# One dK store in two parts, over two DMA queues

## Chip, cores and metric

The kernel runs on one core of a Trainium2 chip. The metric is the device time of one execution in microseconds (us); the median of three runs before the change is 1361.11 us (1361.1 to 1362.07). The core has a matrix engine (PE), a vector engine (DVE), a scalar engine (ACT), GpSimd (POOL) and a sync engine (SP) that here does little but issue transfers. Transfers between HBM and on-chip memory (SBUF, 128 partitions) are moved by 16 DMA engines.

## The reference

One decode step of a transformer block with adaptive layer norm, and its gradients. The part that sets the time is attention of one query per head over a cache: 32 heads, 8192 positions, head size 192, bf16.

```python
scores = jnp.einsum('bhqd,bhkd->bhqk', q, k) * Dh ** (-0.5)
p = _softmax(scores, axis=-1)
o = jnp.einsum('bhqk,bhkd->bhqd', p, v)
...
_out, _vjp = jax.vjp(_f, A_x, A_k_cache, A_v_cache, A_wq, A_wo, B_w3, B_w4, c, w_mod)
_grads = _vjp(grad_out)
```

The outputs include the gradients of both caches, dK and dV, each as large as its cache: 32 heads of 8192 x 192 numbers, 3 MB (3072 KB) per head. Per head dV is the outer product of the probabilities p and the gradient `do` of o, and dK that of dS and q, where dS comes from p and the product of V with `do`. Beside that there are the gradients of the projections `wq` and `wo`, of the MLP's `w3` and `w4`, of the modulation's weights `w_mod`, and three outputs of 640 numbers.

## The kernel before

A head's K, V, dK or dV lies in SBUF as 128 partitions of 64 positions each; one partition's row is 64 x 192 bf16 = 24,576 bytes, and contiguous in HBM. "Half" tiles of 32 positions are used where a buffer is smaller (1536 KB, rows of 12,288 bytes).

The forward stage (to about 545 us) goes over the heads 0 to 31. It loads K and V of each head, computes scores on DVE and PE (`fwd_mult`, `fwd_ssum`), the softmax on ACT and DVE, and sums over the positions on PE. It never normalizes V's product by a second pass: `fwd_kv` keeps matrices (L471, L482) from which the gradient of q is later read. L488 (`fwd_kvK`) multiplies with `hot_bf`, a small constant tile with one column of ones; no line after the forward stage reads it.

A middle stage (545 to 565 us) does the MLP forward and backward; here the DMA queues drain.

The backward stage goes over the heads from 31 down: `HS[i] = 31 - i`, one iteration i of the loop at L1465 per head. V is loaded again (`ring_load`, L880) into one of two places of `v_mem`. In iteration i:

- `bwd_dv` makes dV of the next head: ACT the first 20 positions of each half (L1243), DVE the rest (L1219), then the store at L1265.
- `bwd_mult` multiplies V by `do` on DVE (L131) and sums on PE (L1238).
- `bwd_ds` makes dS, and `bwd_dk` makes dK: two DVE multiplies (L1219) and the store at L1283.
- Jobs are mixed in: gradients of `wo`, `w4`, `w3` (L1301 to L1314) and, over the iterations 10 to 24, of `wq` and `w_mod` (L1332 load, L1354 multiply, L1355 store).

Output tiles of 3 MB take turns in three places A, B and C of `k_mem`; later the places X and V1 join them:

```python
outs += list("BCA") * 11 + ["B"]
outs += ["X", "C", "A", "B"] * 2 + ["X", "C", "V1", "B", (0, 1)]
st2 = nc.sync
```

A place is written again three outputs later, so ACT at L1243 and DVE at L1219 wait until its old content has been stored. All loads and stores of the backward stage are issued by SP, in program order; an SP instruction that waits for its data holds up all later ones. Each DMA marks its completion on one of eight semaphores in turn, and an issue waits until the DMA eight issues earlier has landed.

PE, DVE and ACT run their instructions in the order in which the program emits them (`pin_order`); GpSimd and SP are not pinned, and the recording layer orders them. GpSimd has ten short instructions in the whole kernel; the last two rebuild `sel_bf` (L1460, L1461) after L1206 has read it, for L1130, which first reads it at 610.3 us.

Of the kernel before, what the change touches and what calls it, by code (L numbers as in the profile page):

```python
# [20 lines left out]
def kernel(  # L21
# [26 lines left out]
    nc = tc.nc  # L48
# [16 lines left out]
    P = 128  # L65
# [34 lines left out]
    def bank_c(name):  # L100
        return bank("c", CB[0], name)
# [9 lines left out]
    hot_bf = const.tile([P, 2 * HQ - 1], BF16, name="hot_bf")  # L111
# [78 lines left out]
    def dve_copy(out, in_):  # L190
        nc.vector.tensor_copy(out=out, in_=in_)
# [10 lines left out]
    dK_hd = [out_2[0, h].rearrange("(p j) d -> p j d", p=P) for h in range(HQ)]  # L202
# [449 lines left out]
    for i in range(1, HQ):  # L652
        c, p, pp = 2 <= i < HQ, 0 <= i - 1 < HQ, 0 <= i - 2 < HQ
# [192 lines left out]
    HS = list(range(HQ - 1, -1, -1))  # L846
# [22 lines left out]
    def ring_load(i):  # L869
        if i == 2:  # L870
            load_wo(1, v_tile(bv, 5))
        while v_jobs and all(("v", HS[v_occ[sl][0]], v_occ[sl][1]) in freed for sl in range(v_jobs[0][2], v_jobs[0][2] + v_jobs[0][3])):
            k, t, slot, n = v_jobs.pop(0)
            for r in range(n):
                v_occ[slot + r] = (k, t + r)
            if n == 1:
                V_b.setdefault(HS[k], {})[t] = load_v(fv, HS[k], t, slot)
            else:
                V_b[HS[k]] = {r: v_tile(fv, slot + r) for r in range(2)}
                nc.sync.dma_start(out=v_pair(k), in_=V_hd[HS[k]])  # L880
        for n in W_AT.get(i, ()):
            name, u, use = W_USE[n]
            load_side(name, u, v_tile(bv, 5) if n % 3 == 0 else side["w"].tile([P, JH, DH], BF16, name="W_sb", tag=f"sw{n % 3}"))

    def out_place(k):
        if isinstance(k, tuple):
            return [big_half(x) for x in k], None
        tl = places[k]
        return [tl[:, 0:JH, :], tl[:, JH : 2 * JH, :]], tl
# [15 lines left out]
    st2 = nc.sync  # L905
# [13 lines left out]
    def bwd_pf(h):  # L919
        bwd_pf_act(h)  # L920
        bwd_pf_dve(h)
# [188 lines left out]
    def bwd_wo_red(b):  # L1110
        ps, lo, n = dof_ps.pop(b)
        nc.vector.reduce_sum(out=dof[:, 3 * lo : 3 * (lo + n)], in_=ps, axis=AX.X)
# [7 lines left out]
    def fin_do_sum(b):  # L1120
        lo, n = PS[BATCHES[b][-1]], len(BATCHES[b])
        bwd_wo_red(b)
        sl = slice(3 * lo, 3 * (lo + n))
        dop = bsm.tile([P, 9], BF16, name="dop")[:, 0 : 3 * n]
        dve_copy(dop, dof[:, sl])
        ps = bank_c("dop_ps")
        for k in range(3):
            for c in range(3):
                lo2 = 2 + k * P - c
                nc.tensor.matmul(ps[:, k * n : (k + 1) * n], lhsT=sel_bf[:, lo2 : lo2 + P], rhs=dop[:, c : 3 * n : 3], start=(c == 0), stop=(c == 2))  # L1130
        do_rows[b] = (sl, ps, n)
# [57 lines left out]
    def bwd_dob(hp):  # L1189
        do_pb[hp] = pair_bc(bsm, do_bf, hp, "do_pb")  # L1190
        q_pb[hp] = pair_bc(bsm, q_bf, hp, "q_pb")
# [26 lines left out]
    def pairs_outer(o, pairs, vec, n):  # L1218
        nc.vector.tensor_tensor(  # L1219
            out=o.rearrange("p j (d r) -> p j d r", r=2),  # L1220
            in0=pairs[:, :, None, :].to_broadcast([P, n, NP2, 2]),
            in1=vec.rearrange("p (d r) -> p d r", r=2)[:, None, :, :].to_broadcast([P, n, NP2, 2]),
            op=ALU.mult)

    def vec_of(d, h):
        return d[h // 2][:, (h % 2) * DH : (h % 2 + 1) * DH]

    def bwd_mult(h, t, parts=1):
        if t == 0:
            w = SB[0] // J  # L1230
            bst[h]["dP_ps"] = bank("s", 2, "dP_ps", SB[0]).rearrange("p (j d) -> p j d", d=w)
        w = SB[0] // J
        n = JH // parts
        for r in range(0, JH, n):
            V_sb = V_b[h][t][:, r : r + n, :]
            mul(V_sb, V_sb, vec_of(do_pb, h)[:, None, :].to_broadcast([P, n, DH]))
            for k in range(DH // w):
                nc.tensor.matmul(bst[h]["dP_ps"][:, t * JH + r : t * JH + r + n, :], lhsT=ident_bf, rhs=V_sb[:, :, k * w : (k + 1) * w], start=(k == 0), stop=(k == DH // w - 1))  # L1238
        freed.add(("v", h, t))
# [34 lines left out]
    def bwd_dk(h, t):  # L1274
        if t == 0:
            bst[h]["dk"] = out_place(outs.pop(0))
        halves, whole = bst[h]["dk"]
        j0 = t * JH
        pairs_outer(halves[t], bst[h]["dS2"][:, j0 : j0 + JH, :], vec_of(q_pb, h), JH)
        if whole is None:  # L1280
            st2.dma_start(out=dK_hd[h][:, j0 : j0 + JH, :], in_=halves[t])
        elif t == 1:
            st2.dma_start(out=dK_hd[h], in_=whole)  # L1283

    def job_mid():
        lnb_rest()
        h2 = hc
        mul(h2, n1_c, cb1)
        add(h2, h2, sb)
        add(h2, h2, mid_ps["h2"])  # L1290
        mul(dmod_c[:, 5 * NDC : 6 * NDC], dy_c, h2)
        mul(h2, h2, gb)
        add(h2, h2, x1_c)
        store_cols(out_0[0, 0], h2, const, st2, "x2")
        mul(dmod_c[:, 2 * NDC : 3 * NDC], dx1, ao_c)
        dve_copy(dmod_c[:, 3 * NDC : 4 * NDC], dhb)
        mul(dmod_c[:, 4 * NDC : 5 * NDC], dhb, n1_c)
# [167 lines left out]
    for i in range(HQ):  # L1465
        h, nxt = HS[i], HS[i + 1] if i + 1 < HQ else None
        if i % 2 == 1 and i > NPH and nxt is not None:
            bwd_dob(nxt // 2)
        for f in J0[i]:
            f()  # L1470
        if i <= AHEAD:
            if i in SPLIT:
                bwd_pf(nxt)
            for t in range(2):
                bwd_mult(h, t, 2 if i == 0 else 1)
                if i == t == 0:
                    ring_load(0)
                    c_first = fin_c(PS[0], 1)
                if i == 2 and t == 0:
                    fin_do_out(0)  # L1480
                if i in SPLIT:
                    bwd_dv(nxt, t)
        if i not in EARLY and i <= RING_AT:
            ring_load(i)
        if i - 1 in dq:
            fin_dq(*dq.pop(i - 1))
        if i == 0:
            fin_c_copy(PS[0], 1, c_first)
        if nxt is not None and i not in SPLIT:
            if i > 0:  # L1490
                bwd_pf(nxt)
            for t in range(0 if i > 0 else 1, 2):
                bwd_dv(nxt, t)
        if i in EARLY:
            ring_load(i)
        if i == 0:
            mid_cols()
            perm_cols()
            bwd_ds(h)
            dq_last(h)  # L1500
        if i < NPH:
            hook(i)
        if i == 3:
            bcast_cols(du_bf, 0, NFC, du_bc, act_copy)
        for f in J1[i]:
            f()
        if i > 0:
            bwd_ds(h)
        if i >= AHEAD and nxt is not None:
            for t in range(2):  # L1510
                bwd_mult(nxt, t)
            if i >= RING_AT:
                ring_load(i + 1)
        bwd_dk(h, 0)
        bwd_dk(h, 1)
        while stores:
            stores.pop(0)()
        if i in cps:
            fin_c_copy(*cps.pop(i))
        if i == 1:  # L1520
            fin_do_sum(0)
        if i == MID_AT:
            job_mid()
            dve_copy(dmod_bf[:, 2 * NDC : 6 * NDC], dmod_c[:, 2 * NDC : 6 * NDC])
        if i == NPH - 1:
            fin_dq(*dq.pop(i))
            mm_cm.__exit__(None, None, None)
            psum_cm.__exit__(None, None, None)
            psum[0] = ctx.enter_context(tc.tile_pool(name="psum_s", bufs=1, space=bass.MemoryType.PSUM, reuse_waits="tile"))
            SB[0] = 1024  # L1530
            for nm, b in (("w", 1), ("bcp", 1)):
                side_cm.append(tc.tile_pool(name="side" + nm, bufs=b, side="right", reuse_waits="tile"))
                side[nm] = side_cm[-1].__enter__()
        for f in J2[i]:
            f()
        if i == I_SIDE:
            while side_cm:
                side_cm.pop().__exit__(None, None, None)
            xt = ctx.enter_context(tc.tile_pool(name="xt", bufs=1, side="right", reuse_waits="tile"))
            places["X"] = xt.tile([P, 2 * JH, DH], BF16, name="xt")  # L1540
            for k in range(2):
                places[f"V{k}"] = v_mem[:, 2 * k * JH : 2 * (k + 1) * JH, :]
# [31 lines left out]
```

## Time and profile before

| | |
|---|---|
| median of the runs | 1361.11 us (3 runs, 1361.1 to 1362.07) |
| profiled execution | 1361.22 us |
| its span, first to last instruction | 1359.4 us |
| busy: PE, DVE, ACT, POOL | 64%, 80%, 67%, 0% |
| DMA engines: mean rate, bytes | 418 GB/s, 567.62 MB |
| packets of SP's queue (q1) | 98.8% of 16 engines' span |
| 3 MB loads of V: issue to landing | 18.7 us (median) |
| 3 MB stores from `k_mem`: issue to landing | 27.9 us (median) |

All numbers of one profile come from one execution, so sums over its rows are compared with 1361.22 us. Busy shares are means over stages that have different limits. "DMA share" is the mean busy share of the 16 DMA engines; a value just over 1 comes from packets that overlap slightly in the records. A transfer of 128 rows is cut over the 16 DMA engines, each marks its end by itself, and the transfer has landed when the last of the 16 has; the trace holds the time of each mark, and the start, size and duration of each packet, but not the number of the engine that moved it.

### The profile page before, as it was taken

Reading aid. Unit: us, or ns where it says so; the run is one execution under the profiler, and the core shown is the slowest. Engines: PE = TensorE matmul, PEld = TensorE weight load, DVE = VectorE, ACT = ScalarE, POOL = GpSimd, SP = SyncE. Lnnn points to the kernel's source line nnn. Section 1 sums busy time; section 2 is a strip of 40 time slices with the busy share of each in tenths; the row PEclk is TensorE's granted clock in tenths of the full one; section 3 lists DMA queues with packets and bytes.
Section 4 is the critical chain, followed back from the end, with each engine's and each line's share of the span. In section 5 each row is a group of like instructions: output and inputs, shape, how many; then the busy total and the mean of one; then the engine's idle time right before and its main releaser. Section 6 shows DMA issues by size and latency. Waiting matters only on the chain.

```text
span 1359.4 us, 27668 instructions
## 1 busy us (share of the span) xinstructions
PE 872.6 (64%) x11406; PEld 622.4 (46%) x11406; DVE 1084.0 (80%) x1247; ACT 916.2 (67%) x2558; POOL 3.2 (0%) x10
## 2 busy tenths in 40 slices
PE   4698999999999999848756654434333443243240
PEld 3577777777777777736635541111111111011110
DVE  3488888888888888899878987877668978788783
ACT  0387787778788885876866957765467745667660
POOL 0000000000000000000000000000000000000000
PEclk9799999999999999577676676676666766666665
DMA  9999999999999999799999999999999999999997
GB/s 391 418 422 427 424 416 426 420 412 425 424 418 417 423 424 401 280 397 423 424 426 428 429 428 431 432 430 428 426 428 434 424 428 431 427 430 435 430 432 331
DMA packets 46282, 567.62 MB, mean 418 GB/s; under 512 B 4685, under 2 KB 6989, under 8 KB 19405
## 3 DMA queue, kind: packets, MB, share of 16 engines
q1 hardware_dynamic: 46126, 565.86, 98.8%
q8 instruction: 89, 1.46, 0.4%
q14 instruction: 37, 0.30, 0.1%
q10 hardware_dynamic: 30, 0.00, 0.0%
HBM read 339.94 MB, written 225.91 MB: 416 GB/s over the span
## 4 chain that ended last, share of the span: by engine, by line
DMA 48%; PE 22%; DVE 20%; ACT 3%; SPq 2%; issue 2%; DVEq 0%; ACTq 0%
DMA out_dram<-k_mem 25%; DMA v_mem<-in_A_v_cache_dram 18%; DVE k_mem L1219 10%; PE ps_a L471 7%; PE dP_ps L1238 4%; DVE v_mem L131 4%; PE ps_b L482 4%; DMA k_mem<-in_A_k_cache_dram 3%; PE S_ps L411 2%; ACT k_mem L1243 2%; DMA out_dram<-dw 2%; PE kb_ps L488 2%; SPq L234 1%; DVE prod L131 1%; DVE V_sb L131 1%
## 5 line engine op out<-in xcount | busy, mean ns | idle before, releaser
L1243 ACT ACTIVATE k_mem<-do_pb,PF 128x192 bf16<-128x192 bf16 x1086 | 379.9, 454 | 131.0 <-DMA out_dram<-k_mem 90.9
L1238 PE MATMUL dP_ps<-v_mem,ident_bf 128*128 128x512 bf16 (+2 forms) x960 | 223.5, 408 | 251.8 <-DVE v_mem L131 251.7
L446 ACT ACTIVATE EK<-k_mem,E_f 128x192 bf16<-128x192 bf16 x992 | 355.6, 446 | 36.6 <-issue 19.3
L1238 PEld LDWEIGHTS <-ident_bf 128*128 128x128 bf16 x1056 | 121.2, 120 | 368.8 <-DVE v_mem L131 197.7
L1219 DVE TENSOR_TENSOR k_mem<-dS,q_pb 128x6144 bf16<-128x6144 bf16 x64 | 212.2, 3354 | 52.7 <-DMA out_dram<-k_mem 52.3
L131 DVE TENSOR_TENSOR v_mem<-v_mem,do_pb 128x6144 bf16<-128x6144 bf16 (+1 forms) x62 | 199.1, 3249 | 21.4 <-DMA v_mem<-in_A_v_cache_dram 21.4
L131 DVE TENSOR_TENSOR prod<-k_mem,q_pb 128x6144 bf16<-128x6144 bf16 x62 | 207.7, 3350 | 4.7 <-DMA k_mem<-in_A_k_cache_dram 3.5
L471 PE MATMUL ps_a<-EK,v_mem 128*128 128x193 bf16 x1984 | 191.6, 248 | 15.8 <-DMA v_mem<-in_A_v_cache_dram 15.7
L471 PEld LDWEIGHTS <-v_mem 128*128 128x128 bf16 x1984 | 163.7, 98 | 34.2 <-DMA v_mem<-in_A_v_cache_dram 19.5
L453 DVE TENSOR_TENSOR EK<-k_mem,P2h 128x1536 bf16<-128x1536 bf16 x124 | 117.9, 951 | 0.0
L482 PE MATMUL ps_b<-EK,v_mem 128*64 128x193 bf16 x1984 | 106.7, 249 | 0.0
L411 PE MATMUL S_ps<-prod,ident_bf 64*64 64x256 bf16 x2976 | 95.8, 275 | 7.2 <-DVE prod L131 7.2
L411 PEld LDWEIGHTS <-ident_bf 64*64 64x64 bf16 x3072 | 84.9, 110 | 26.5 <-issue 24.4
L482 PEld LDWEIGHTS <-v_mem 128*64 128x64 bf16 x1984 | 79.9, 109 | 19.1 <-issue 15.5
L1219 DVE TENSOR_TENSOR k_mem<-P2h,do_pb 128x2304 bf16<-128x2304 bf16 (+2 forms) x56 | 74.3, 1358 | 12.3 <-DMA out_dram<-k_mem 11.5
L488 PE MATMUL kb_ps<-EK,hot_bf 128*32 128x384 bf16 x992 | 63.5, 333 | 0.0
L188 ACT CAST do_pb<-bc_ps 128x384 bf16<-128x384 f32 x15 | 7.2, 479 | 79.8 <-PE bc_ps L184 79.8
L451 DVE CAST EK<-E_f 128x16 bf16<-128x16 f32 x124 | 24.5, 197 | 32.3 <-ACT EK L446 22.7
L432 ACT ACTIVATE E_f<-sm_ps,negm 128x64 f32<-128x64 f32 x31 | 9.8, 315 | 58.6 <-DVE negm L430 58.6
L415 DVE TENSOR_REDUCE S<-S_ps 128x128 f32<-128x1024 f32 x32 | 39.2, 1225 | 11.0 <-PE S_ps L411 10.8
L1347 PEld LDWEIGHTS <-ident_bf 128*128 128x128 bf16 x100 | 11.8, 118 | 73.8 <-issue 68.3
L1243 ACT ACTIVATE xt<-do_pb,PF 128x192 bf16<-128x192 bf16 x120 | 41.9, 457 | 3.1 <-DMA out_dram<-xt 3.1
(340 smaller groups left out, 835.2 us busy)
## 6 DMA issues: line engine op xcount, KB each, us to landing
v_mem<-in_A_v_cache_dram SPq DMA_DIRECT2D x47, 3072.0 KB, 18.7
out_dram<-k_mem SPq DMA_DIRECT2D x42, 3072.0 KB, 27.9
k_mem<-in_A_k_cache_dram SPq DMA_DIRECT2D x20, 3072.0 KB, 14.3
out_dram<-k_mem SPq DMA_DIRECT2D x33, 1536.0 KB, 21.5
v_mem<-in_A_v_cache_dram SPq DMA_DIRECT2D x25, 1536.0 KB, 20.4
k_mem<-in_A_k_cache_dram SPq DMA_DIRECT2D x24, 1536.0 KB, 19.0
out_dram<-xt SPq DMA_DIRECT2D x3, 3072.0 KB, 22.3
wq<-in_A_wq_dram SPq DMA_DIRECT2D x3, 2560.0 KB, 33.9
```

Source lines behind the costliest of these rows:

```text
L131: nc.vector.tensor_tensor(out=out, in0=a, in1=b, op=ALU.mult)
L411: nc.tensor.matmul(st["S_ps"][c0 : c0 + 64, r, t * JH : (t + 1) * JH, :], lhsT=ident_bf[64 * r : 64 * r + 64, 64 * r : 64 * r + 64], rhs=p ...
L415: nc.vector.reduce_sum(out=st["S2"], in_=st["S_ps"], axis=AX.X)
L446: nc.scalar.activation(out=st["EK"][q][:, jj, 0:DH], in_=K_st[h, t][:, r * JQ + jj, :], func=ACT.Copy, scale=st["E_f"][:, j : j + 1])
L451: nc.vector.tensor_copy(out=EK[:, :, DH : DH + 1], in_=st["E_f"][:, q * JQ : (q + 1) * JQ, None])
L453: nc.vector.tensor_tensor(out=EK[:, NA:JQ, 0:DH].rearrange("p j (d r) -> p j d r", r=2), in0=K_st[h, t][:, r * JQ + NA : (r + 1) * JQ, :]. ...
L471: nc.tensor.matmul(st["A_ps"][:, 0:n], lhsT=V_sb[:, r * JQ + jj, a0:a1], rhs=EK[:, jj, 0:n], start=(q == 0 and jj == 0), stop=(q == 3 and ...
L482: nc.tensor.matmul(st["B_ps"][g : g + 64, 0:n], lhsT=V_sb[:, r * JQ + jj, b0:b1], rhs=EK[:, jj, 0:n], start=(q == 0 and jj < 2), stop=(q = ...
L488: nc.tensor.matmul(kb_ps[g : g + 32, 0 : 2 * DH], lhsT=hot_bf[:, HQ - 1 - h : 2 * HQ - 1 - h], rhs=EK[:, jj : jj + 2, 0:DH], start=(h == 0 ...
L1219: nc.vector.tensor_tensor(out=o.rearrange("p j (d r) -> p j d r", r=2), in0=pairs[:, :, None, :].to_broadcast([P, n, NP2, 2]), in1=vec.rea ...
L1238: nc.tensor.matmul(bst[h]["dP_ps"][:, t * JH + r : t * JH + r + n, :], lhsT=ident_bf, rhs=V_sb[:, :, k * w : (k + 1) * w], start=(k == 0), ...
L1243: nc.scalar.activation(out=o[:, jj, :], in_=vec_of(do_pb, h), func=ACT.Copy, scale=bst[h]["PF"][:, t * JH + jj : t * JH + jj + 1])
```

## The change

The dK store of one head (iteration i = 22, head 9) is issued in two parts. Partitions 0 to 119 are issued by GpSimd, with a limit of 12,288 bytes per piece, so that each row of 24,576 bytes goes in two; by the change's description they run over 15 DMA engines. Partitions 120 to 127 stay with SP. Two small loads are added on GpSimd, of 5 and of 12 rows of `B_w4` (two pieces of 8 numbers per row), into `hot_bf`, which nothing reads any more. In the code they stand in the iterations 14 and 28; in GpSimd's built order both stand ahead of the memset of `sel_bf`, and the store stands last. The second load waits for the first (both write the same tile).

```diff
         if whole is None:
             st2.dma_start(out=dK_hd[h][:, j0 : j0 + JH, :], in_=halves[t])
+        elif t == 1 and h == HS[PART_AT]:
+            nc.gpsimd.dma_start(out=dK_hd[h][0:120], in_=whole[0:120], max_dma_last_dim=12288)
+            st2.dma_start(out=dK_hd[h][120:P], in_=whole[120:P])
         elif t == 1:
             st2.dma_start(out=dK_hd[h], in_=whole)
+
+    PART_AT = 22
+
+    def turn_engines(k):
+        def part(x):
+            return x[0:k, 0:32].rearrange("p (b c) -> p b c", b=2)[:, :, 0:8]
+
+        nc.gpsimd.dma_start(out=part(hot_bf), in_=part(B_w4))
...
         if i == 1:
             fin_do_sum(0)
+        if i == PART_AT - 8:
+            turn_engines(5)
+        if i == PART_AT + 6:
+            turn_engines(12)
         if i == MID_AT:
             job_mid()
```

The order of PE, DVE, ACT and SP is unchanged; SP's 8-row store stands where the whole store stood.

## The prediction

> **What bounds the kernel now.** I read the page first (busy shares, slices, DMA queues), then the chain of waits, then stretches of the second half, and last the final 20 us by windows, since a shared resource shows its limit where it drains.
>
> The page's slices and queues:
>
> ```profile
> DMA  9999999999999999799999999999999999999997
> ...
> q1 hardware_dynamic: 46126, 565.86, 98.8%
> q8 instruction: 89, 1.46, 0.4%
> q14 instruction: 37, 0.30, 0.1%
> ```
>
> The DMA engines are full in every slice but two; no computing engine is over 80%. One queue, q1, which the sync engine (SP) fills, holds nearly all bytes. The chain's last 120 us say the same:
>
> ```profile
> 1137.26 31.68 DMA out_dram<-k_mem
> ...
> 1176.11 33.70 DMA v_mem<-in_A_v_cache_dram
> ...
> 1240.42 37.50 DMA out_dram<-k_mem
> ...
> 1284.67 37.37 DMA out_dram<-k_mem
> ...
> 1333.68 3.27 DVEq L1569
> ```
>
> A 3 MB transfer (3072 KB) at the 430 GB/s of this stretch takes 3.146 MB / 430 GB/s = 7.3 us, and here it needs 31 to 37 us from issue to landing. So some 20 us of older transfers stand ahead of each one. The backward stage waits on a backlog, not on latency: whoever is late by a few us finds the engines still supplied.
>
> Now the end, by windows (us; then PE, PEld, DVE, ACT, POOL busy; clock; DMA share; GB/s):
>
> ```profile
> 1336.00:1341.00 5.00, 0.00 (x0) 0.00 (x0) 0.95 (x1) 0.00 (x0) 0.00 (x0) 0.50 1.03 442
> 1346.00:1349.00 3.00, 0.00 (x0) 0.00 (x0) 0.00 (x0) 0.00 (x0) 0.00 (x0) 0.50 1.00 426
> 1349.00:1350.70 1.70, 0.00 (x0) 0.00 (x0) 0.00 (x0) 0.00 (x0) 0.00 (x0) 0.50 0.61 260
> 1350.70:1353.00 2.30, 0.00 (x0) 0.00 (x0) 0.00 (x0) 0.00 (x0) 0.00 (x0) 0.50 0.43 182
> 1353.00:1355.40 2.40, 0.00 (x0) 0.00 (x0) 0.00 (x0) 0.00 (x0) 0.00 (x0) 0.50 0.25 108
> 1355.40:1358.10 2.70, 0.00 (x0) 0.00 (x0) 0.00 (x0) 0.00 (x0) 0.00 (x0) 0.50 0.05 23
> ```
>
> This is the finding that the forecast rests on. The share falls from 1.00 in steps: 0.25 of 16 engines is four, and 0.05 is one. The 16 engines do not finish together: the first are done near 1349, four work until 1355.4, and **one engine alone works for the last 2.7 us**. The completion marks of the last store (16, one per engine) say it too: 9.1 us from first to last, the last three before the end within 0.05 us of each other and 2.8 us ahead of the very last. Going back, that gap is no accident of the end: the spread of the marks is 0.15 us at 567 us, 3.4 at 660, 5.4 at 975, 7.6 at 1137 and 9.1 at the end. One engine has a little more to do in all of the backward stage and falls behind. From 650 us on the DMA share of every 100 us window is 1.00 or 1.01, so none of them runs dry.
>
> So the span ends when the slowest engine has moved its share, and each engine's sum of bytes is the quantity to count. Three stores of five rows (the outputs of 640 numbers) run on five engines only. Their five packets of 256 B begin in the last one at 1224.48, 1224.54, 1226.14, 1230.29 and 1232.33 us: the lags of the big transfers around them (7.9 us from first to last). The slowest engine is one of those five; so are one of the 2.8 us trio and three faster ones. The store at 766 us and the one at 1015 us show their last packet equally late, so it is the same engine throughout.
>
> **The change, part by part.** Sums are made against the profiled execution: 1361.22 us, a span of 1359.4 and 1.8 around it. The median of the runs shown is 1361.11.
>
> Removed: of the dK store of head 9 (i = 22), issued by SP at 1152.99, the rows 0 to 119. Each of the 16 engines moved 8 rows of 24,576 B of it, 196,608 B. At 430 GB/s / 16 = 26.9 GB/s per engine a row takes 0.914 us, the eight 7.3 us.
>
> Added, first: 120 rows from GpSimd over 15 engines, 8 rows each: 7.3 us on 15 engines, nothing on the sixteenth. The rows come in pieces of 12,288 B. The stretch with such rows (650 to 850 us) ran at 426 to 429 GB/s, later ones at 427 to 432: under 1% of 7.3 us, below 0.1 us, which may be of either sign.
>
> Added, second: 8 rows from SP. Eight rows give at most eight engines one row each: +0.91 us on eight engines. The five-row stores went to five engines, the slowest among them; I take the eight to contain these five. Bounds: 0 (they miss the slowest) and 7.3 us (all eight rows on the slowest, which the five-row stores, spread over five engines, speak against).
>
> So per engine: the one left out has 7.3 us less, or 6.4 if it also gets one row; up to eight have 0.91 us more; the rest have nothing new. No byte is saved. The time changes only by which engine is left out.
>
> Added, third: two loads on GpSimd, of 5 and 12 rows, a few dozen bytes per row, into hot_bf, whose last reader is the matmul group of L488 (last start 545.4 us). In GpSimd's own order both stand ahead of the memset of sel_bf, which begins at 565.44, once L1206 is done. The three loads of 1.2 KB at the start landed 1.3, 4.6 and 4.9 us after issue; two in series, since the second waits for the first, take 10 us of those 20. If that cover were gone, the next is 45 us: L1130 first reads sel_bf at 610.3. Cost nothing; they move no weight on any engine either.
>
> The wait that moves: GpSimd now waits for the DVE multiplies of dK (L1219), as SP does; nothing is queued behind it on GpSimd. SP still waits there for its 8 rows, so the V_sb store at 1154.69 and the v_mem load at 1155.11 keep their place. Readers of the buffer wait for both parts:
>
> ```profile
> 1177.33 2.63 DVE L1219 TENSOR_TENSOR k_mem<-P2h,do_pb 128x2304 bf16<-128x2304 bf16 x2 [1.53 <-DMA out_dram<-k_mem]
> 1177.40 13.96 ACT L1243 ACTIVATE k_mem<-do_pb,PF 128x192 bf16<-128x192 bf16 x40 [11.16 <-DMA out_dram<-k_mem]
> ```
>
> The old store landed at 1175.73 with those two waiting. The new part has a queue of its own and no longer stands behind SP's 17 us of backlog; shared evenly it lands about 2 x 7.3 us after issue, near 1168. In return the dV store of 1137.26, which landed at 1168.94 and released dK's next multiplies at 1169.04, lands up to 7.3 us later. At that moment the engines hold work until 1187 (first) to 1195 us (last), so the DVE can be 7.3 us late at 1183 and none runs dry; later transfers keep their order and find each engine with the same sum behind it. Taken as nothing; if that cover failed, 7.3 us at most, once.
>
> When does GpSimd start? The trace has no DMA from it. Bounds: SP's own 0.33 us, and the next DVE pause, 1159.5 to 1161.6, if GpSimd had to wait for that: 7 us late and landed by 1175, still in time. [...]
>
> **Rivals and numbers.** 0.2% is 2.7 us, about what a measurement of this kernel can tell from no change.
>
> *A, the forecast: the left-out engine is not the slowest, so the change does not do what leaving one out could do.* Then the slowest keeps its 8 rows and gains one: 1361.22 + 0.9 = 1362.1. Own range 1361.2 (no row for it) to 1362.6. For it: 15 of 16 engines, or 4 of the 5, are the wrong one, and nothing in the trace names them. Chance 0.55.
>
> *B: it is the slowest.* It ends 6.4 us earlier and is last no more; the trio ends 2.7 us before the old end, and the member that is among the five gains 0.9. 1361.22 - 2.7 + 0.9 = 1359.4; without that row 1358.5. More than 2.7 us is not to be had. For it: the slowest is one of only five, and the 5 and 12 rows feed nothing, so all they can set is which engines the store gets; against it: four of the five are wrong, and so are the eleven others. I take a little over one in five: chance 0.25, of which 0.10 reaches beyond 0.2%. [...]
>
> *C, slower: GpSimd's pieces occupy an engine longer than SP's.* Nearest row: the instruction queue q8, 0.4% of 16 x 1359.4 us for 89 packets, is 0.98 us per 16.4 KB, where q1's rate gives 0.61, 1.6 times as long. At that ratio 7.3 us become 11.7 on each of the 15 engines: 1362.1 + 4.4 = 1366.5. From 0.11 us extra on each of 16 pieces it exceeds 2.7 us together with the row of A. Against it: SP's own pieces of this size cost nothing extra. Chance 0.20.
>
> A and B lie within 0.2% but for 0.10 of B; C is slower. Faster 0.10, same 0.70, slower 0.20. The range takes B from its low end through A and the nearest part of C: 1358.4 to 1363.4.
>
> **What would show it.** Right: the DMA share stays at 1.00 after 1160; the last windows still end with one engine alone for about 2.7 us or a little more, 0.9 us later. B: the lone tail is gone, and the share ends in steps of three. C: the new queue's share per byte is above q1's. Wrong altogether: a window after 1160 with a share under 0.95 (engines run dry, the handover cost something), or a lone tail that moved by more than 2 us in either direction without that.

## The result and the profile after

The changed kernel takes 1366.78 us (median of 6 runs, 1366.53 to 1369.33) beside 1361.11 of the kernel before (6 runs on the same chip): a ratio of 1.0046, 95% interval 1.0034 to 1.0059. It is slower by 5.7 us, outside the forecast range. (Ratios and intervals, here and below, are estimated from the single runs, so a ratio can differ a little from the quotient of the medians.) The profiled execution took 1368.37 us, with a span of 1366.6; the span before was 1359.4, so 7.2 us are to be found in the trace.

Up to 1155 us the rates of the two traces agree. The stretches behind that, of the kernel after (us; busy PE, PEld, DVE, ACT, POOL; clock; DMA share; GB/s):

```profile
1155.00:1160.00 5.00, 0.00 (x0) 0.00 (x0) 3.99 (x5) 5.00 (x16) 0.00 (x0) 0.50 1.03 400
1160.00:1165.00 5.00, 0.00 (x0) 0.00 (x0) 2.11 (x1) 5.00 (x16) 0.00 (x0) 0.50 0.96 307
1165.00:1170.00 5.00, 3.70 (x11) 1.44 (x12) 4.51 (x2) 0.68 (x3) 0.00 (x0) 0.59 0.99 309
1170.00:1175.00 5.00, 3.02 (x15) 1.18 (x12) 0.00 (x0) 0.00 (x0) 0.00 (x0) 1.00 0.99 287
1175.00:1180.00 5.00, 0.00 (x0) 0.00 (x0) 2.08 (x1) 0.00 (x0) 0.00 (x0) 0.59 1.02 345
1180.00:1185.00 5.00, 0.00 (x0) 0.00 (x0) 4.78 (x4) 0.02 (x1) 0.00 (x0) 0.50 1.02 346
1185.00:1190.00 5.00, 0.00 (x0) 0.00 (x0) 4.55 (x5) 5.00 (x15) 0.00 (x0) 0.50 0.97 401
1190.00:1200.00 10.00, 1.07 (x3) 0.43 (x4) 4.49 (x2) 8.90 (x26) 0.00 (x0) 0.50 1.01 433
```

Three of the same stretches of the kernel before:

```profile
1160.00:1165.00 5.00, 0.02 (x1) 0.02 (x2) 3.43 (x2) 5.00 (x16) 0.00 (x0) 0.50 1.02 436
1165.00:1170.00 5.00, 5.00 (x12) 1.77 (x13) 4.16 (x2) 1.24 (x4) 0.00 (x0) 0.50 0.99 419
1170.00:1175.00 5.00, 2.83 (x13) 1.08 (x11) 5.00 (x2) 0.00 (x0) 0.00 (x0) 0.99 0.99 425
```

Read the last two columns together. The DMA share stays near 1.00, as forecast; nothing runs dry. But from 1160 to 1185 us the same busy engines move 287 to 346 GB/s where they moved 418 to 436 before. The seven stretches to 1190 us miss 615 GB/s x 5 us = 3.1 MB against 430 GB/s, and 3.1 MB at 430 GB/s are 7.2 us: the whole loss lies in these 35 us. A full share beside a low rate means that each packet lasts longer, and that this time counts as busy (from 1170 to 1175 us SP's 24,576-byte packets take 1438 ns on average, at a share of 0.99).

The new queue on the page and its DMA issue, and in the second block the two queues between 1155 and 1185 us (packets, MB, share of 16 engines; q1 is SP's queue, q0 GpSimd's):

```profile
q1 hardware_dynamic: 45998, 562.91, 98.1%
q0 software_dynamic: 336, 2.95, 0.7%
...
out_dram<-k_mem POOLq DMA_DIRECT2D x1, 2880.0 KB, 31.7
```

```profile
q1 hardware_dynamic: 547, 6.99, 67.7%
q0 software_dynamic: 272, 2.95, 32.2%
```

GpSimd's store needs 31.7 us to land, not the 15 forecast. Of 16 x 30 us, 32.2% for 2.95 MB are 52 us of one engine per MB on GpSimd's queue, and 67.7% for 6.99 MB are 46 on SP's. At 430 GB/s / 16 it would be 37. **Both queues are slow**. The packet records say the same: in the seven stretches to 1190 us SP's 24,576-byte packets average 949 to 1438 ns (the longest takes 3309), against 913 to 940 before, where most take 912. GpSimd's 12,288-byte pieces average 474 to 673 ns in the stretches to 1180 us, though many of them take 460.

The chain of waits shows where the lateness enters:

```profile
1153.11 31.59 DMA out_dram<-k_mem
1184.70 0.21 SPq L1286
...
1185.00 33.23 DMA v_mem<-in_A_v_cache_dram
...
1340.87 3.27 DVEq L1584
```

The V load that SP issued at 1176.11 before goes out at 1185.00, 8.9 us late, and the chain stays 7 to 9 us late to the end. The chain puts this down to GpSimd's store, but SP's store ahead of the load was issued at 1184.58, before that store had landed. SP's store had waited for the dK multiplies, which ended at 1184.55; here they are in the kernel after, then before:

```profile
1177.92 6.63 DVE L1219 TENSOR_TENSOR k_mem<-dS,q_pb 128x6144 bf16<-128x6144 bf16 x2 [8.41 <-DMA out_dram<-k_mem]
```

```profile
1169.04 6.63 DVE L1219 TENSOR_TENSOR k_mem<-dS,q_pb 128x6144 bf16<-128x6144 bf16 x2 [0.84 <-DMA out_dram<-k_mem]
```

They waited for the dV store of 1136.72, which landed at 1177.83 instead of 1168.94: one of the older transfers that the new store jumped ahead of and slowed. The backlog covers the late issue (the share is 0.97 and 1.01 in the stretches behind it), so it follows from the loss and is not a second one. The end:

```profile
1350.00:1354.00 4.00, 0.00 (x0) 0.00 (x0) 0.00 (x0) 0.00 (x0) 0.00 (x0) 0.50 0.98 418
1354.00:1360.00 6.00, 0.00 (x0) 0.00 (x0) 0.00 (x0) 0.00 (x0) 0.00 (x0) 0.50 0.61 260
1360.00:1367.00 7.00, 0.00 (x0) 0.00 (x0) 0.00 (x0) 0.00 (x0) 0.00 (x0) 0.50 0.12 51
```

The lone tail of 2.8 us is gone, but not because its engine was spared. The last store's 16 completion marks stand 11.6, 11.0, 10.8, 10.4 ... 3.2, 2.4, 1.1 and 0 us ahead of the end: the slow stretch delayed the engines by different amounts and shuffled them. In the transfers that land from 1190 to 1225 us one engine's mark stands alone at the head, 13.7 us ahead of the last where the next is 11.0 ahead: the engine left out. The first of the five-row store's packets (1227.01 us; the others from 1233.64 on) stands at this engine's mark of the transfer before (1227.37, the next one 1230.0). So it is one of the five engines of the five-row stores, and a leading one: case A's branch.

Two quantities describe the kernels below: the **shortage** (bytes missing from 1150 to 1215 us against 430 GB/s, as time) and the **mean idle time** of the 16 engines at the end, from the marks of the last store. Before: 0.2 and 6.2 us. After: 7.0 and 6.6, so 1359.4 + 6.8 + 0.4 = 1366.6, the span. For the other kernels with both quantities in the table the same sum comes within 1.3 us of the span of the profiled execution.

### The profile page after: what moved, and what is told of

Its sections match the earlier page's. It is cut to its first block, busy times and chain, and to the rows that moved or that the text cites. A ratio compares the mean times of both kernels' runs of the same rounds, so it can differ in the third digit from the quotient of the medians.

```text
span 1366.6 us, 27677 instructions
## 1 busy us (share of the span) xinstructions
PE 867.6 (63%) x11406; PEld 620.1 (45%) x11406; DVE 1083.9 (79%) x1247; ACT 913.4 (67%) x2558; POOL 5.7 (0%) x13
## 3 DMA queue, kind: packets, MB, share of 16 engines
q0 software_dynamic: 336, 2.95, 0.7%
## 4 chain that ended last, share of the span: by engine, by line
DMA 47%; PE 23%; DVE 22%; SPq 2%; issue 2%; ACT 2%; DVEq 0%; ACTq 0%; POOLq 0%
DMA out_dram<-k_mem 25%; DMA v_mem<-in_A_v_cache_dram 17%; DVE k_mem L1219 10%; PE ps_a L471 8%; DVE v_mem L131 5%; PE ps_b L482 4%; PE dP_ps L1238 3%; DMA V_sb<-in_w_mod_dram 3%; PE S_ps L411 3%; PE kb_ps L488 2%; DVE prod L131 1%; DMA k_mem<-in_A_k_cache_dram 1%; SPq L234 1%; DVE V_sb L131 1%; ACT k_mem L1243 1%
## 5 line engine op out<-in xcount | busy, mean ns | idle before, releaser
L1238 PE MATMUL dP_ps<-v_mem,ident_bf 128*128 128x512 bf16 (+2 forms) x960 | 220.1, 404 | 260.7 <-DVE v_mem L131 260.5
```

## The experiments

Theory 1 was formed from this trace: both queues are slow at once (52 and 46 us of one engine per MB, where 430 GB/s would be 37), and the change cuts the store by rows. It says that a cut by rows gives the engines other rows of the SBUF tile than an uncut store, and that engines with such rows then wait for each other, whichever queue their packets come from. This is the author's estimate of the cause: no view of the trace shows which rows an engine takes or what an engine waits for. The rivals blame GpSimd's queue or two queues on one engine (2), SP's eight rows (3), the store's jump ahead of older transfers (4), or the places of the rows in HBM (5); that an engine of the changed kernel has eight neighbouring rows, as rival 5 takes it, is an estimate too (120 rows on 15 engines).

The edits are made to the changed kernel, and those with stores stand in `bwd_dk`. The two small loads are left out, except in the run without SP's eight rows and in the section on the left-out engine, which says where they stay.

The shortage and the idle time are those of one profiled execution each.

| kernel | us, median | before, same chip | ratio, 95% interval | shortage, us | mean idle at end, us |
|---|---|---|---|---|---|
| whole store from GpSimd | 1360.69 | 1360.71 | 0.9999 (0.9990 to 1.0008) | 0.4 | 5.8 |
| 120 + 8 rows, both from SP | 1369.49 | 1360.71 | 1.0060 (1.0048 to 1.0073) | 5.0 | 9.1 |
| without SP's 8 rows | 1366.67 | 1360.71 | 1.0042 (1.0029 to 1.0055) | 6.3 | 7.7 |
| 112 rows on 16 engines + 16 | 1366.75 | 1360.71 | 1.0044 (1.0030 to 1.0057) | 5.8 | 5.9 |
| eight parts by columns | 1361.25 | 1360.77 | 1.0003 (0.9994 to 1.0012) | 0.8 | 6.4 |
| eight parts of 16 rows | 1372.84 | 1360.77 | 1.0084 (1.0070 to 1.0098) | 11.2 | 5.6 |
| eight parts, every 8th row | 1372.01 | 1360.77 | 1.0081 (1.0068 to 1.0094) | 14.9 | 1.9 |
| four parts of 32 rows | 1367.06 | 1360.63 | 1.0046 (1.0034 to 1.0059) | 7.0 | 4.8 |
| whole store, spread in HBM | 1361.07 | 1360.63 | 1.0003 (0.9994 to 1.0012) | 0.1 | 7.0 |
| without the load of 12 rows | 1366.81 | 1360.63 | 1.0045 (1.0031 to 1.0058) | 7.4 | 3.6 |
| loads in the code's order | 1365.87 | 1360.66 | 1.0043 (1.0030 to 1.0055) | 7.9 | 3.5 |
| last half store split | 1361.88 | 1360.63 | 1.0011 (1.0003 to 1.0020) | | |
| the same, with 12 rows behind | 1362.70 | 1360.66 | 1.0013 (1.0004 to 1.0022) | | |

### The queue, the split, the eight rows, the left-out engine

The whole store from GpSimd, on 16 engines:

```diff
-            nc.gpsimd.dma_start(out=dK_hd[h][0:120], in_=whole[0:120], max_dma_last_dim=12288)
-            st2.dma_start(out=dK_hd[h][120:P], in_=whole[120:P])
+            nc.gpsimd.dma_start(out=dK_hd[h], in_=whole, max_dma_last_dim=12288)
```

> All 128 rows of the store from GpSimd over 16 engines, in the same 12,288-byte pieces; no store by the sync engine, no small loads. [...] Rival 2 (GpSimd's queue, or two queues taking turns on an engine, is slow in itself): the same loss or more, 128/120 of 5.7 us: 1367. Rival 4 (the store jumps ahead of older transfers, and the late dV store costs the time): the same loss, 1367.

Of this kernel, stretches as above, then the two queues between 1155 and 1185 us:

```profile
1160.00:1165.00 5.00, 0.00 (x0) 0.00 (x0) 3.11 (x1) 5.00 (x16) 0.00 (x0) 0.50 0.97 417
1165.00:1170.00 5.00, 4.70 (x15) 1.87 (x16) 3.51 (x2) 0.18 (x1) 0.00 (x0) 0.65 1.00 421
1170.00:1175.00 5.00, 2.19 (x11) 0.78 (x8) 1.49 (x1) 0.00 (x0) 0.00 (x0) 1.00 1.07 455
```

```profile
q1 hardware_dynamic: 657, 9.54, 75.6%
q0 software_dynamic: 272, 3.15, 24.7%
```

The same queue, pieces and jump ahead, on 16 engines and not cut by rows: no loss, as theory 1 expects. Both queues take 38 us of one engine per MB, and GpSimd's pieces 460 to 464 ns on average. Rivals 2 and 4 fall, and with them case C's mechanism. This run also shows that lateness alone costs nothing: the dV store landed at 1173.42 (before: 1168.94) and SP's V load went out at 1180.59 (before: 1176.11), both 4.5 us late, without a loss of time.

The split of 120 and 8 rows, both parts from SP:

```diff
-            nc.gpsimd.dma_start(out=dK_hd[h][0:120], in_=whole[0:120], max_dma_last_dim=12288)
+            st2.dma_start(out=dK_hd[h][0:120], in_=whole[0:120], max_dma_last_dim=12288)
```

> The same split, 120 rows and 8 rows, but both parts issued by the sync engine on its one queue; no small loads. [...] Rival 2 (GpSimd's queue or two queues on an engine): no loss, 1361 to 1362 (plus up to 0.9 us for one more row on the slowest engine; or, if the engine left out is the slowest, up to 2.7 us less). Rival 4 (jumping ahead): no loss either, since the order is that of before.

```profile
1160.00:1165.00 5.00, 0.00 (x0) 0.00 (x0) 3.29 (x2) 5.00 (x16) 0.00 (x0) 0.50 1.03 377
1165.00:1170.00 5.00, 4.87 (x15) 1.89 (x16) 3.34 (x2) 1.37 (x5) 0.00 (x0) 0.62 0.98 313
1170.00:1175.00 5.00, 2.26 (x11) 0.82 (x9) 0.45 (x1) 0.00 (x0) 0.00 (x0) 1.00 0.99 315
```

One queue, no GpSimd, no jump, and the rate falls all the same. At +8.8 us the loss is above the 5.7 of the change: the shortage is smaller (5.0 us beside 7.0), but the engines' idle time at the end grows to 9.1 us, with the last engine 5.3 us behind the next.

The changed kernel without SP's eight rows, which are then never written:

```diff
-            st2.dma_start(out=dK_hd[h][120:P], in_=whole[120:P])
+            pass
```

> The changed kernel without the sync engine's 8 rows (rows 120 to 127 of this one head's dK are not written). Theory 1: the loss is nearly whole, 1366 less about 0.9 us for the row that the slowest engine no longer gets. [...]

The loss stays whole (+6.0 us): the eight rows do not cause it (rival 3), nor does leaving them out show up as a gain of 0.9 us.

112 rows from GpSimd and 16 from SP:

```diff
-            nc.gpsimd.dma_start(out=dK_hd[h][0:120], in_=whole[0:120], max_dma_last_dim=12288)
-            st2.dma_start(out=dK_hd[h][120:P], in_=whole[120:P])
+            nc.gpsimd.dma_start(out=dK_hd[h][0:112], in_=whole[0:112], max_dma_last_dim=12288)
+            st2.dma_start(out=dK_hd[h][112:P], in_=whole[112:P])
```

> GpSimd stores rows 0 to 111 over 16 engines, 7 rows each, in the same pieces; the sync engine stores rows 112 to 127, one row per engine; no small loads. No engine is left out and every engine moves the same bytes as before. [...] If the loss comes from leaving an engine out (15 of 16 engines carry the same bytes): none, 1361 to 1362. Rivals 2 and 4: 112/120 of the loss, about 5.3 us, 1366.

```profile
1170.00:1175.00 5.00, 2.19 (x11) 0.78 (x8) 0.00 (x0) 0.00 (x0) 0.00 (x0) 1.00 1.00 275
```

All 16 engines are to have the same bytes as before (7 rows and 1; the author's count, no view shows it for this run), and the loss is there (+6.0 us). If the count holds, it is not the left-out engine either. What the losing runs have in common, and the whole store has not, is the cut by rows.

### SBUF or HBM, and the dose

Each of these edits replaces the two stores of the change. First eight parts by columns:

```diff
+            for k in range(8):
+                nc.gpsimd.dma_start(out=dK_hd[h][:, 8 * k : 8 * k + 8, :], in_=whole[:, 8 * k : 8 * k + 8, :])
```

> The store in eight parts from GpSimd, each of all 128 rows and an eighth of the columns (3,072 B per row). [...] It is the control for the two runs beside it: theory 1 expects 1361 within 1.5 us. If the number of transfers on GpSimd's queue, or their smaller packets, cost time, it shows here.

Eight parts of 16 neighbouring rows:

```diff
+            for k in range(8):
+                nc.gpsimd.dma_start(out=dK_hd[h][16 * k : 16 * k + 16], in_=whole[16 * k : 16 * k + 16], max_dma_last_dim=12288)
```

> The store in eight parts from GpSimd, each of 16 neighbouring rows, one row per engine, all 16 engines used. [...] Rival 5 (the cause lies in HBM, where the engines of the changed kernel read or write eight rows, 196,608 B, apart): here they write neighbouring rows, so no loss like it, below 1364.

Eight parts with every eighth row:

```diff
+            for k in range(8):
+                nc.gpsimd.dma_start(out=dK_hd[h][k:P:8], in_=whole[k:P:8], max_dma_last_dim=12288)
```

> As the run beside it, but each part has every eighth row: again 16 rows, one per engine, the same bytes and pieces. [...] Theory 1: 14.6 us instead of 7.3, a loss of 5 to 9 us as with the 120 rows, 1366 to 1370, and at most half of the loss of the 16 neighbouring rows. Rival 5 (HBM): the engines write eight rows apart as in the changed kernel, so its loss or more, and more than with neighbouring rows.

Four parts of 32 neighbouring rows, a size between the parts of 16 rows and the whole store:

```diff
+            for k in range(4):
+                nc.gpsimd.dma_start(out=dK_hd[h][32 * k : 32 * k + 32], in_=whole[32 * k : 32 * k + 32], max_dma_last_dim=12288)
```

> The store in four parts from GpSimd, each of 32 neighbouring rows, two per engine, all 16 engines used. [...] Theory 1: between the two, a loss of 5 to 9 us, 1366 to 1370, and a rate between 1155 and 1185 us between that of the 16 rows (234 to 340 GB/s) and 430. Rival (every mapping but the usual costs the same): 1372 as with the 16 rows.

Stretches of the 16 neighbouring rows, then of the four parts of 32, then of every eighth row:

```profile
1165.00:1170.00 5.00, 4.66 (x11) 1.65 (x12) 3.56 (x2) 0.00 (x0) 0.00 (x0) 0.50 0.95 238
1170.00:1175.00 5.00, 3.62 (x14) 1.34 (x12) 0.00 (x0) 0.00 (x0) 0.00 (x0) 0.87 1.04 235
```

```profile
1165.00:1170.00 5.00, 5.00 (x16) 1.92 (x17) 3.17 (x1) 0.00 (x0) 0.00 (x0) 0.67 0.96 266
1170.00:1175.00 5.00, 1.92 (x9) 0.69 (x7) 0.00 (x0) 0.00 (x0) 0.00 (x0) 1.00 0.99 287
```

```profile
1165.00:1170.00 5.00, 0.00 (x0) 0.00 (x0) 0.00 (x0) 1.43 (x5) 0.00 (x0) 0.50 0.97 314
1170.00:1175.00 5.00, 0.00 (x0) 0.00 (x0) 0.00 (x0) 0.00 (x0) 0.00 (x0) 0.50 1.00 318
...
1185.00:1190.00 5.00, 0.00 (x0) 0.00 (x0) 4.42 (x5) 4.50 (x13) 0.00 (x0) 0.50 0.49 211
```

By columns, in eight transfers with 512 packets of 6,144 bytes, nothing is lost (the interval spans no change). With 16 neighbouring rows the loss is 12.1 us, with 32 neighbouring rows 6.4 us: twice the rows in a part and about half the loss.

The run with every eighth row missed its expected 1366 to 1370 us, and its time says little about what such rows cost. Between 1185 and 1190 us the share falls to 0.49: the engines run dry. The waits name the cause:

```profile
DVE k_mem L1219 <- DMA out_dram<-k_mem: 30.5, 1, 30.5
```

DVE stood 30.5 us at one multiply until GpSimd's store had landed, against 12.4 us in three waits with the 16 neighbouring rows; why it had to wait for those rows I have not settled. Its first five stretches, still full, can be read: from 1155 to 1180 us they miss 2.0 MB, 4.7 us. The 16 neighbouring rows miss 4.1 MB, 9.5 us, in the same stretches, the 32 rows 2.6 MB, 6.0 us, and the changed kernel 2.5 MB, 5.8 us. That is the order which theory 1 expected of this run (at most half of the loss of the 16 neighbouring rows) and the opposite of what rival 5 expected: parts with rows 196,608 B apart in HBM cost less than parts of neighbours.

The 14.6 us in place of 7.3 that theory 1 gave for such rows are the author's estimate; no run shows the factor of two. In the runs the 32 rows and the change itself show 6.8 us (7.0 less the 0.2 of before), the 16 neighbouring rows 11.0.

HBM by itself: the whole store from GpSimd, written to every second row of the dK of heads 9 and 10 (the output is wrong in those two heads):

```diff
+            two = out_2[0, h : h + 2].rearrange("h (p j) d -> (h p) j d", p=P)
+            nc.gpsimd.dma_start(out=two[0 : 2 * P : 2], in_=whole, max_dma_last_dim=12288)
```

> [...] Theory 1 (SBUF side): 1361 within 1 us, rate above 410 GB/s throughout. Rival 5 (HBM side): a loss like the changed kernel's, 1366 to 1368.

```profile
1165.00:1170.00 5.00, 4.30 (x13) 1.68 (x14) 3.90 (x2) 0.52 (x2) 0.00 (x0) 0.61 0.97 409
1170.00:1175.00 5.00, 2.61 (x13) 0.98 (x10) 1.10 (x1) 0.00 (x0) 0.00 (x0) 1.00 1.08 460
```

No loss with the rows 49,152 B apart in HBM instead of 24,576 (1.0003; a shortage of 0.1 us), where rival 5 expected 1366 to 1368 us. How far apart in HBM the engines write at one time, here or in the runs that are cut by rows, no view shows. So HBM is not excluded for those runs, and a share of their loss could lie there.

### Which engine is left out, and what that is worth

The next run is the kernel before, with one of the outputs of 640 numbers stored as 4 + 1 rows in `store_cols` and one as 3 + 2:

```diff
-        eng.dma_start(out=dram_row.rearrange("(i p) -> i p", p=P), in_=rb)
+        cut = {"x0o": 4, "dco": 3}.get(name, NDC)
+        for r0, r1 in ((0, cut), (cut, NDC)):
+            if r1 > r0:
+                eng.dma_start(out=dram_row.rearrange("(i p) -> i p", p=P)[r0:r1], in_=rb[r0:r1])
```

> The kernel before, with two of its three outputs of 640 numbers stored in two parts (4 + 1 rows and 3 + 2 rows instead of 5), to see how far each of the five engines lags. [...] No theory turns on it; time as before, 1361 within 2 us. [...]

It took 1360.27 us in its one run. The four rows landed at 1015.02, 1015.02, 1016.01 and 1017.77 us, the single one at 1015.20. In the kernel before, the five landed at 1015.82 to 1021.17. So the transfer of four rows misses the slowest engine and the one of five has it (last landings at 1017.77 and 1021.17 us). That the loads ahead of the store set which engine it leaves out is the author's supposition. In the order of the code the 5 rows would come before the store and the 12 after it; in the built order both come before.

So the next two runs change what stands ahead of the store and aim at leaving out the slowest engine. The trace numbers no engine: the "low engines" of the expectations are the five of the five-row stores, "engine 4" is the slowest of them. The first is the changed kernel without the load of 12 rows, the second keeps both loads and pins GpSimd to the order of the code:

```diff
-            turn_engines(12)
+            pass
```

> [...] Theory 1: the slow-down of both queues stays (5.7 us), but the end loses the lone tail of 2.7 us, less up to 0.9 us for the row that others of the low engines gain: 1364 to 1365.5, and no single mark far behind the others at the end. [...]

```diff
-            if not seen or ins.engine not in (mybir.EngineType.PE, mybir.EngineType.DVE, mybir.EngineType.Activation):
+            if not seen or ins.engine not in (mybir.EngineType.PE, mybir.EngineType.DVE, mybir.EngineType.Activation, mybir.EngineType.Pool):
```

> The changed kernel with GpSimd's instructions pinned to the order of the code: the load of 5 rows, the store of 120, then the load of 12. [...]

In a store over 15 engines GpSimd's queue has 32 entries of 4 bytes, 17 more than one mark for each of the 15; the whole store on 16 engines has 16. A row of these entries stands one SP packet apart (0.914 us), and is taken as that of the left-out engine. In the second kernel SP's mark between two of them is written at 1161.15 us; the V load's marks land until 1161.51, the last of 16. By this the left-out engine is the slowest. In the profiled execution of the first kernel it is too (1160.35, last of 16 at 1160.83). The end of the second:

```profile
1354.00:1358.00 4.00, 0.00 (x0) 0.00 (x0) 0.00 (x0) 0.00 (x0) 0.00 (x0) 0.50 0.86 366
1358.00:1361.00 3.00, 0.00 (x0) 0.00 (x0) 0.00 (x0) 0.00 (x0) 0.00 (x0) 0.50 0.41 176
1361.00:1363.00 2.00, 0.00 (x0) 0.00 (x0) 0.00 (x0) 0.00 (x0) 0.00 (x0) 0.50 0.09 37
```

The share stays high for longer, and the mean idle time falls from 6.6 us in the changed kernel to 3.5; in the first it is 3.6. The times hardly follow. The first took 1366.81 us (1364.83 to 1367.42), where 1364 to 1365.5 was expected; the second 1365.87, beside an estimate of 1360.7 + 7.0 - 2.7 = 1365 (the time before, the shortage of the change, the lone tail). The changed kernel took 1366.78. The shortage rose to 7.4 and 7.9 us in these executions, and the ratios (1.0045 and 1.0043) cannot be told from that of the change (1.0046). A better balance by 3 us is seen in the marks of one execution each; in the medians no gain is shown. That the same engine is left out in every execution is not shown either.

Last, the same idea at the end, where the DMA share of the kernel before falls from 0.61 (1349 us) to 0.05 (1355.4 us). GpSimd is pinned as above, the store of i = 22 is whole and from SP, and the load of 5 rows stays; the second kernel has `turn_engines(12)` behind the store:

```diff
+        if whole is None and t == 1 and h == HS[-1]:
+            nc.gpsimd.memset(v_mem[:, 2 * JH, 0:8], 0.0)
+            nc.gpsimd.dma_start(out=dK_hd[h][0:120, j0 : j0 + JH, :], in_=halves[t][0:120])
+            st2.dma_start(out=dK_hd[h][120:P, j0 : j0 + JH, :], in_=halves[t][120:P])
```

> [...] GpSimd first clears a few numbers of the place V1 of v_mem, so it starts only once the store of that place has landed (1344 us), when most engines are nearly idle. Theory 1 with engine 4 as the slowest: it ends 3.65 us earlier, plus 0.46 for its one row; the engines 2.8 us ahead of it become the last, plus up to 0.46 us: 1358.5 to 1359.5. Rivals: the split costs its usual share even there (half of 5.7 us), 1361 or more; or GpSimd starts too late and the end is that of its own part, 1362 or more.

> [...] In the run before, the slowest engine did get rows of GpSimd's part (its mark of the store ahead came 3.1 us later than in the kernel before), so another engine was left out. Theory 1 with engine 4 as the slowest: its last mark comes 3.65 us earlier, plus 0.46 for one row; the next engines, 2.8 us ahead of the old end, become the last, plus up to 0.5 us: 1358.3 to 1359, faster than the kernel before by 0.15 to 0.2%. [...]

Both lost: 1361.88 us beside 1360.63 and 1362.70 beside 1360.66, where 1358.5 to 1359.5 and 1358.3 to 1359 were expected. Of the second:

```profile
1346.00:1349.00 3.00, 0.00 (x0) 0.00 (x0) 0.00 (x0) 0.00 (x0) 0.00 (x0) 0.50 1.04 336
1349.00:1351.00 2.00, 0.00 (x0) 0.00 (x0) 0.00 (x0) 0.00 (x0) 0.00 (x0) 0.50 0.92 289
```

Busy engines move 336 and 289 GB/s: the low rate is there too, though half the engines were to be idle. Two engines write their last mark of SP's store ahead at 1359.4 and 1359.6 us, 4.5 us later than that store's end before (1354.9). Which engine was left out in this kernel is not settled, and neither is whether the low rate is the whole loss. No version beat the kernel before. By the marks of the kernel before, leaving out the slowest engine can give 2.7 us at most, and the price of doing it by a split of a 3 MB store was 7 us of shortage.

## Why the prediction was wrong, point by point

- **What bounds the kernel**: right. The DMA engines are full, and the end is set by the sum of each engine's work. Only, that sum is not one of bytes alone (287 to 346 GB/s at a share of 0.96 to 1.02 from 1160 to 1185 us).
- **"Each of the 16 engines moved 8 rows ... 7.3 us on 15 engines"**: this is the step that failed. A row was priced at 0.914 us whichever engine takes it, and so "the time changes only by which engine is left out". The price holds for the store that is not cut by rows (whole store from GpSimd: 0.4 us of shortage). With 120, 112 or 32 rows per transfer, from either queue, the 16 engines together lost 5.0 to 7.9 us, SP's packets among them; in the changed kernel 7.0. Of that failure the cut by rows is shown to be the cause; how it slows the packets is not shown.
- **8 rows from SP, +0.91 us**: no such term shows; without them the loss is 6.0 us beside 5.7.
- **Pieces of 12,288 B**: right, 460 to 464 ns each on average with the whole store.
- **The small loads cost nothing, and `sel_bf` is not late**: right; its memset begins at 564.73 (before: 565.44), and the loads took 0.69 and 0.56 us of GpSimd.
- **GpSimd's start, the landing "near 1168", the hand-over "taken as nothing"**: the issue began at once (1153.11), but the first packet began only at 1157.69 and the last part landed at 1184.7. Even without a loss the landing was priced too low: the whole store from GpSimd needed 23.2 us, not 15. The dV store of 1137.26, allowed to be "up to 7.3 us" late, was 8.9 late. The hand-over itself cost nothing, since no stretch of 5 us to 1190 us, and none of 10 us from there to 1350, has a share under 0.95. (The old dK store, said to have landed at 1175.73, has its last mark at 1177.24; nothing in the sum hangs on it.)
- **Case A**: its branch came true (a leading engine was left out), its time did not, by 4.7 us. **Case B**: in the profiled executions of two runs the slowest engine was left out; the lone tail went, the loss stayed. **Case C**: its 1366.5 is near the measured 1366.78 by luck. Its reason, pieces that take longer on GpSimd's queue alone, is wrong: SP's queue slows down as well (46 us per MB of one engine, 38 with the whole store), and the same pieces over 16 engines do not. "Slower" had a chance of 0.20 for that reason alone.
- **"What would show it"** looked at the share per byte of one queue and at the share of the stretches. GB/s beside a full share was the column to name.

## What to carry to other kernels

Where the DMA engines are the bound as here, keep transfers of all 128 partitions whole, or split them by columns. A split by columns cost nothing here (a ratio of 1.0003, 0.9994 to 1.0012); splits of one 3 MB store by rows cost 6 to 12 us, on either queue. Read GB/s beside the DMA share: full engines that moved fewer bytes spent longer on each packet (949 to 1438 ns beside 913 to 940). A gain by balancing engines has to be set against the price of the odd transfer that brings it, and here it was the smaller of the two.

## What the runs showed that I had not expected

- Busy DMA engines moved 287 GB/s, and 235 with 16 neighbouring rows, beside 430.
- GpSimd's first packet began 4.6 us after the issue (5.4 with the whole store). No run shows what it waited for.
- The store of 120 rows put 32 entries of 4 bytes on GpSimd's queue, the whole store 16. By the count above 17 of the 32 are those of the sixteenth engine, one SP packet (0.914 us) apart.
- With GpSimd's loads in the built order a leading engine was left out, with those of the code's order the slowest (one execution each): the order in which a program is built can decide what such a trick does.
